# Set attention and a gated feed-forward on one core: block 0's second product in undivided float32, and one more super-block turned on the chip

## The chip, the cores and the metric

The kernel runs on one core of one Trainium2 chip. The metric is the device time of one execution in microseconds (us); before the change it is 1614.46 us, the median of three runs.

## What is computed

Four sets of 12480 points with 128 channels go through an attention with 32 inducing points, twice, and the result goes through a feed-forward layer with 2048 hidden channels:

```python
def mab(q, kv):
    s = scale * (q @ kv.transpose(0, 2, 1))
    s = s - s.max(-1, keepdims=True)
    a = np.exp(s)
    a /= a.sum(-1, keepdims=True) + 1e-09
    return a @ kv
h = mab(I, x)                      # I: inducing points, (4, 32, 128)
x = mab(x, h).reshape(4 * 12480, 128)
h = x @ w_in                       # w_in: (128, 2048)
g = h * (1.0 / (1.0 + np.exp(-1.702 * h)))
out = g @ w_out                    # w_out: (2048, 128)
```

The points and the inducing points are float32; w_in and w_out come as float64, and the kernel turns them into float32 itself.

## The kernel before

**Tiles.** A set is cut into six super-blocks of 2048 points (s = 0 to 5) and a rest of 192 (s = 6). A whole super-block holds four blocks of 512 points. The feed-forward layer goes by blocks: 98 in all, two of them made of the rests of two sets. A block has eight groups (`NG`), each of two chunks of 128 hidden channels.

**The feed-forward layer.** `first(i)` does group i: two float32r products into one `ph` buffer in PSUM (there are two), then the gated activation on ACT into `g`. It then divides `g` into `hi`, which is float32r, and the rest `lo`, so that products of full precision can be had from float32r: `hi` is made by ACT from `ph` again or by DVE from `g`, `lo` by DVE. `second(i, c)` does one chunk of the second product, three float32r products into the block's `pso`: `hi` with `wl`, `lo` with `wh`, `hi` with `wh`. w_out was divided in the same way into `wh` and `wl`. After a block's last chunk ACT copies `pso` to `ob`, which SP stores. Up to seven groups are ahead of the second product (`LAG`).

**The start.** `start` does the first attention of set 0 and the decoding of the weights, before the first block:

- The scores of super-block s (`scores`, PE) are copied by ACT, their maxima taken by DVE, then `softmax` makes the exponentials on ACT and their transposes `aT` on DVE. `weighing` multiplies `aT` by the rows of x, 16 products for a super-block. The rows come in two ways: for s below `XB` = 4, `turning` turns the columns that are there already (`xt`) by 16 transposes on PE into `ph` and two ACT copies into `xf`; for s = 4, 5 and 6 they are loaded from `in_x` a second time, as `xf`, `xn` (line 707, `x5`) and `xf_last`.
- After `weighing`, `joining` sums up (`hu`, `hT`), `first_weights` does the second attention of block 0 (`e`, `sm`, `two`, a turn of four float32r matmuls by `ident_r`, `st`), and `h_w_in` makes the four quarters of `hw`, the product of `hT` with w_in. Three more such turns (`more_weights`) make `st` for blocks 1 to 3.
- w_in and w_out are decoded in quarters of 512 columns by `decode_in` and `decode_out`: bit operations on DVE, two conversions on ACT. `decode_out` puts out `wh` (rounded by ACT) and `wl` (DVE). The quarters 2 and 3 of w_out are loaded when the weighing of super-block 5 has freed their buffer.
- `spin` fills PE's gaps with matmuls whose result nobody reads (`spun`).

**What sets the order.** The program is written once, for all engines, in an order that `Jobs` and `Clocks` choose when the kernel is built: each pending step has an engine and tiles, and the step that can begin first by modelled costs comes next, with a rank as a handicap. What they choose is fixed in the program; on the chip each engine goes through its own list in order and waits for what an instruction needs. In the main loop at the end, `begin_group` says whether the next group or the next chunk of the second product comes next, and `in_time` how much left-over work may be fitted in; DVE's share of decoding w_out is measured out by `progress` and `DECODE`.

The second product of block 0 needs the quarter of w_out for its chunk (`decoded`):

```python
pe_.matmul(o, wlc, hi[:, c, :], start=(ch == 0), stop=False)
pe_.matmul(o, whc, lo[:, c, :], start=False, stop=False)
pe_.matmul(o, whc, hi[:, c, :], start=False, stop=(ch == NCH - 1))
```

Line 112 of the profile is the helper that records every instruction, so that nearly all have that line; the operations are told apart by the tiles' names.

Of the kernel before, what the change touches and what calls it, by code (L numbers as in the profile page):

```python
# [9 lines left out]
F32 = mybir.dt.float32  # L10
# [12 lines left out]
LAG = 14  # L23
ROOM = 3000.0
LOAD = 400.0
WC = 512
DECODE = 7
ES = 4
XB = 4
FB = 5  # L30
# [86 lines left out]
class Queue(Meter):  # L117
# [3 lines left out]

    def dma_start(self, out, x):
        self.t = self.clocks.begin(self, [out], [x]) + self.cost("dma_start", out, x)
        self.moved = max(self.moved, self.t) + math.prod(out.shape) * 4 / LOAD
        self.clocks.end(self, self.moved + self.after, [out], [x])
        return self.eng.dma_start(out, x)

# [42 lines left out]
def set_attention_then_moe(ctx: ExitStack, tc, xT, x, indT, w_in, w_out, outT):  # L170
# [51 lines left out]
    sups.append((t0, RG, (N - t0) // RG))  # L222
    NS = len(sups)
    EB = NS + 2

    const = ctx.enter_context(tc.tile_pool(name="const", bufs=1))
    px = ctx.enter_context(tc.tile_pool(name="px", bufs=XB))
# [27 lines left out]
    act.activation(warm, one, AF.Exp)  # L255

    w_in_sb = [const.tile([P, WC], F32, name=f"w_in{c}") for c in range(DFF // WC)]
    wh = [const.tile([P, WC // P, P], F32R, name=f"wh{c}") for c in range(DFF // WC)]
    wl = [const.tile([P, WC // P, P], F32R, name=f"wl{c}") for c in range(DFF // WC)]

    xts = {}
# [77 lines left out]
    def first_products(a, s):  # L339

        t0, g, w = sups[s]
        pa = ps_a.tile([P, 512], F32, tag="pa", name="pa")
        xg = xts[a.b, s][:, 0:g * w]
        if a.b == 0 and s < XB:
# [325 lines left out]
    jobs = Jobs(clocks)  # L670
    used = {"pa": 0, "ph": 0, "po": 0}
    done = set()
    progress = [0]

    def has(*what):
        return lambda: all(x in done for x in what)
# [7 lines left out]
    def start(pf, pw):  # L684
# [25 lines left out]
        for s in range(XB, NS):  # L710
            if s == XB:
                t = pf.tile([P, BLK, P], F32, tag="xf", name="xf", bufs=FB)
            elif s < NS - 1:
                t = x5
            else:
                t = pf.tile([P, sups[s][2] // 32, P], F32, tag="xf_last", name="xf_last")
            turned[s] = load_x(0, s, t)
# [22 lines left out]
            act.activation(t.bitcast(F32), t, AF.Copy, scale=factor)  # L740
            done.add(name)

        def rounded(name, out, t):
            yield act, [t], None
            act.copy(out, t.bitcast(F32))
            done.add(name)

        def decode_in(c, t, m):
            raw = raws[c]
            h, l = bits(raw)  # L750
            jobs.add(size(("size in", c), t, raw))
# [4 lines left out]
            jobs.add(to_float(("fraction", c), m, 2.0 ** -30))  # L756
            yield from exponent(("size in", c), t, raw, 0x3F800000)
            yield dve, [m], has(("fraction", c))
            dve.scalar_tensor_tensor(
                w_in_sb[c], m.bitcast(F32), 1.0, t.bitcast(F32), op0=ALU.add, op1=ALU.mult  # L760
            )
            done.add(("w_in", c))

        def decode_out(c, raw, t, m, p):
            h, l = bits(raw)
            whc, wlc = [x[c].rearrange("p c d -> p (c d)") for x in (wh, wl)]
            jobs.add(size(("size out", c), t, raw), 1)
            yield dve, [raw], None
            progress[0] += 1
            dve.tensor_scalar(m, h, 0x1FF, 12, op0=ALU.bitwise_and, op1=ALU.logical_shift_left)  # L770
            yield dve, [raw], None
            progress[0] += 1
            dve.scalar_tensor_tensor(m, l, 20, m, op0=ALU.logical_shift_right, op1=ALU.bitwise_or)
            jobs.add(to_float(("rest", c), m, 2.0 ** -32), 1)
            yield from exponent(("size out", c), t, raw, 0x3FFFF000)
            progress[0] += 3
            jobs.add(rounded(("top", c), whc, t), 1)
            yield dve, [t], None
            progress[0] += 1
            dve.tensor_scalar(p, t, -(1 << 23), None, op0=ALU.bitwise_and)  # L780
            yield dve, [m], has(("rest", c), ("top", c))
            dve.tensor_mul(wlc, m.bitcast(F32), p.bitcast(F32))
            progress[0] += 1
            done.add(("w_out", c))

        def decodes_in():
            temps = [pst.tile([P, TOK], I32, tag="st", name="tmp") for _ in range(4)]
            for c in range(DFF // WC):
                yield from decode_in(c, *temps[c % 2 * 2:c % 2 * 2 + 2])

        def decodes_out():
            temps = [phw.tile([P, WC], I32, tag="hw", name="tmp") for _ in range(3)]
            for c in range(DFF // WC):
# [3 lines left out]
                yield from decode_out(c, raws[DFF // WC + c], *temps)  # L797


        def scores(s):  # L800
# [17 lines left out]
        def turning(s, k0):  # L818

            yield pe_, [xts[0, s]], bank("ph")  # L820
            if k0 == 0:
# [43 lines left out]
        def weighing():  # L865
            for some, at in ((range(ES), 0), (range(ES, NS), P)):
                i = 0
                for s in some:
                    what = [("aT", s)] + [("turned", s, k) for k in (0, 8) if s < XB]
# [159 lines left out]
    def first(i):  # L1029
# [24 lines left out]
    def second(i, c):  # L1054
# [8 lines left out]
        wlc, whc = [x[ch // 4][:, ch % 4] for x in (wl, wh)]  # L1063
        pe_.matmul(o, wlc, hi[:, c, :], start=(ch == 0), stop=False)
        pe_.matmul(o, whc, lo[:, c, :], start=False, stop=False)
        pe_.matmul(o, whc, hi[:, c, :], start=False, stop=(ch == NCH - 1))
        if ch == NCH - 1:
# [52 lines left out]
        late[0] = False  # L1120
        return weights_of(*key), key

    def decoded(ch):
        return ("w_out", ch // 4) in done

    def begin_group(i):

# [3 lines left out]
            return True  # L1131
        at, c = under_way[0]
        ch = 2 * (at % NG) + c
        if not decoded(ch):
            return True
        soon = clocks.free("ph", 2)
        return soon <= pe_.t or soon <= clocks.ready(*parts[at], wh[ch // 4], wl[ch // 4])

    def in_time(eng):

        if eng is dve and progress[0] < (i + 1) * DECODE // 2:
            return math.inf
        return act.t + 500 if eng is act else pe_.t

    i = 0
    while i < n or under_way:
# [2 lines left out]
            pass  # L1149
        if not begin_group(i):  # L1150
            at, c = under_way.pop(0)
            while not decoded(2 * (at % NG) + c):
                jobs.step(but=pe_)
            second(at, c)
        else:
# [55 lines left out]
```

## Time and profile before

| | |
|---|---|
| median of three runs (lowest, highest) | 1614.46 us (1612.99, 1615.7) |
| the profiled execution | 1611.53 us |
| its span, first to last instruction | 1609.5 us |
| PE busy | 1585.7 us, 99% of the span |
| DVE, ACT busy | 1328.2, 1365.1 us (83%, 85%) |
| mean granted clock of PE | 0.995 of full |
| chain that ended last | PE 93%, ACT 1%, DVE 1% |

PE is TensorE, DVE is VectorE, ACT is ScalarE, SP the engine that issues the DMAs. The granted clock is what the chip let TensorE have, as a share of 2.4 GHz. A matmul of float32 stands in the profile as two records, one of float32r as one; they overlap in the pipeline, so what one costs is read from start to start.

### The profile page before, as it was taken

What the parts mean: (1) busy time and instruction counts of PE and PEld (TensorE: products, weight loads), DVE (VectorE), ACT (ScalarE), POOL (GpSimd) and SP (SyncE); (2) the same over time, 40 slices, a digit from 0 to 9 for tenths busy, and PEclk for the clock granted to TensorE, in tenths of its full rate; (3) what the DMA queues carried; (4) which work ended last, traced back from release to release, by engine and by line L of the source; (5) the groups of instructions that cost most, each with busy time, mean ns of one, the idle gap of its engine ahead of it and who ended that gap; (6) DMA issues with size and microseconds to landing.
All of it is one profiled execution on the core that took longest, in us unless ns stands there. A gap on an engine that the chain in (4) does not pass through costs nothing.

```text
span 1609.5 us, 21978 instructions
## 1 busy us (share of the span) xinstructions
PE 1585.7 (99%) x7840; PEld 1238.5 (77%) x7840; DVE 1328.2 (83%) x1526; ACT 1365.1 (85%) x1572; POOL 0.7 (0%) x6
## 2 busy tenths in 40 slices
PE   8799999999999999999999999999999999999999
PEld 7567777777687877777777777777778788888887
DVE  6789787788888888788887987878878888888886
ACT  5589998988798888988798988888888988888885
POOL 0000000000000000000000000000000000000000
PEclk9899999999999999999999999999999999999999
DMA  9111504741223013650414210761211011011100
GB/s 293 53 53 53 180 18 87 174 105 53 91 92 142 30 40 78 170 123 15 123 37 151 77 33 25 173 148 46 77 65 48 19 40 47 30 37 40 37 30 20
DMA packets 87355, 126.76 MB, mean 79 GB/s; under 512 B 12241, under 2 KB 54993, under 8 KB 81617
## 3 DMA queue, kind: packets, MB, share of 16 engines
q1 hardware_dynamic: 87248, 125.37, 28.1%
q8 instruction: 64, 1.05, 0.3%
q14 instruction: 43, 0.34, 0.1%
HBM read 72.11 MB, written 25.56 MB: 61 GB/s over the span
## 4 chain that ended last, share of the span: by engine, by line
PE 93%; ACT 1%; DVE 1%; issue 0%; ACTq 0%
PE pso L112 67%; PE ph L112 23%; PE pa L112 4%; ACT g L112 0%; ACT L112 0%; DVE lo L112 0%; ACT hi L112 0%; ACT e L112 0%; DVE hi L112 0%; DVE tmp L112 0%; ACT tmp L112 0%; DVE e L112 0%; ACT ob L112 0%; ACT wh L112 0%; ACTq L112 0%
## 5 line engine op out<-in xcount | busy, mean ns | idle before, releaser
L112 DVE TENSOR_TENSOR lo<-g,hi 128x1024 fp32r<-128x1024 f32 (+1 forms) x784 | 948.9, 1217 | 166.6 <-ACT hi L112 153.3
L112 ACT ACTIVATE g<-ph 128x1024 f32<-128x1024 f32 (+1 forms) x784 | 810.2, 1038 | 184.8 <-PE ph L112 108.1
L112 PE MATMUL pso<-hi,wl 128*128 128x512 f32 (+1 forms) x1568 | 623.8, 398 | 8.5 <-DVE wl L112 8.5
L112 PE MATMUL pso<-lo,wh 128*128 128x512 f32 (+1 forms) x1568 | 617.6, 394 | 1.2 <-DVE lo L112 1.1
L112 PE MATMUL pso<-hi,wh 128*128 128x512 f32 (+1 forms) x1568 | 617.9, 394 | 0.0
L112 ACT ACTIVATE hi<-ph 128x1024 fp32r<-128x1024 f32 (+1 forms) x497 | 512.8, 1032 | 0.0
L112 PE MATMUL ph<-st,hw 128*128 128x512 f32 x1536 | 481.1, 397 | 4.1 <-ACT hi L112 3.1
L112 PEld LDWEIGHTS pso<-hi,wl 128*128 128x128 f32 x1568 | 295.2, 188 | 91.0 <-issue 11.2
L112 PEld LDWEIGHTS ph<-st,hw 128*128 128x128 f32 x1536 | 286.9, 188 | 84.1 <-ACT g L112 8.8
L112 PEld LDWEIGHTS pso<-hi,wh 128*128 128x128 f32 x1568 | 295.3, 188 | 70.2
L112 PEld LDWEIGHTS pso<-lo,wh 128*128 128x128 f32 x1568 | 294.8, 188 | 70.6 <-DVE lo L112 3.2
L112 DVE CAST hi<-g 128x1024 fp32r<-128x1024 f32 (+1 forms) x287 | 197.1, 687 | 81.2 <-ACT g L112 79.6
L112 ACT COPY ob<-pso 128x512 f32<-128x512 f32 (+1 forms) x98 | 59.3, 605 | 16.0 <-PE pso L112 16.0
L112 ACT ACT_TABLE_LOAD x30 | 38.5, 1283 | 1.3 <-PEq L1201 0.7
L112 PE MATMUL pa<-xt,hT 128*32 128x512 f32 x192 | 24.4, 600 | 1.7 <-DVE e L112 1.6
L979 PEld LDWEIGHTS spun<-ident 128*128 128x128 f32 x150 | 19.6, 205 | 6.3 <-issue 5.0
L112 PE MATMUL pa<-xt,indT_sb 128*32 128x512 f32 x192 | 23.7, 600 | 0.0
L979 PE MATMUL spun<-ident 128*128 128x128 f32 x150 | 22.1, 296 | 1.4 <-POOL ident masks.py:199 1.4
L112 PEld LDWEIGHTS pa<-xn,aT 128*32 128x32 f32 (+1 forms) x594 | 15.1, 109 | 7.7 <-issue 6.2
L112 PE MATMUL pa<-xn,aT 128*32 128x128 f32 (+1 forms) x594 | 20.7, 276 | 0.0
L112 ACT ACTIVATE e<-e 128x512 f32<-128x512 f32 (+1 forms) x28 | 14.5, 573 | 6.4 <-DVE e L112 6.4
L112 ACT ACTIVATE s<-s,nmx 128x512 f32<-128x512 f32 (+1 forms) x28 | 18.5, 663 | 1.0 <-DVE nmx L112 0.9
(91 smaller groups left out, 366.4 us busy)
## 6 DMA issues: line engine op xcount, KB each, us to landing
xt<-in_xT SPq DMA_DIRECT2D x44, 1024.0 KB, 7.1
out_T<-ob SPq DMA_DIRECT2D x96, 256.0 KB, 2.0
xn<-in_x SPq DMA_DIRECT2D x76, 256.0 KB, 5.5
st<-ahT SPq DMA_DIRECT2D x184, 64.0 KB, 2.0
st<-alT SPq DMA_DIRECT2D x184, 64.0 KB, 2.0
raw<-in_w_in SPq DMA_DIRECT2D x4, 512.0 KB, 8.5
raw<-in_w_out SPq DMA_DIRECT2D x4, 512.0 KB, 11.7
hw<-th SPq DMA_DIRECT2D x24, 64.0 KB, 2.0
```

Source lines behind the costliest of these rows:

```text
L112: return f(*a, **k)
L979: nc.tensor.matmul(spun[:, 0:P], ident, ident, start=True, stop=True)
```

## The change

Two things change. The rows of super-block 5 are made by `turning` too, with the transposes on PE and the copies on ACT, into the same buffer (`x5`); its second load from `in_x` goes. And the first eight groups (`WHOLE` = 8, all of block 0) keep `g` as it is, in float32, and multiply it by `whole`, a float32 w_out, in one float32 matmul. w_out is decoded like w_in (one `decode` for both), and `split` divides it into `wh` and `wl` afterwards, quarter by quarter: ACT rounds `whole` into a temporary, DVE subtracts it for `wl`, ACT writes `wh` into the buffer of a `whole` that block 0 has done with. Beside these, the modelled rate of loads of rows is lower (`ROWS`), the products of w_in are ranked later one by one, and `in_time` no longer measures out DVE's steps.

```diff
+    on_chip = [s for s in range(NS - 1) if s != XB]
...
-    wh = [const.tile([P, WC // P, P], F32R, name=f"wh{c}") for c in range(DFF // WC)]
+    pww = ctx.enter_context(tc.tile_pool(name="pww", bufs=DFF // WC))
+    whole = {}
+    wh = {}
...
             elif s < NS - 1:
-                t = x5
+                continue
...
-        def decode_out(c, raw, t, m, p):
...
+        def decode(name, out, raw, t, m, rank):
             h, l = bits(raw)
+            jobs.add(size(("size", name), t, raw), rank)
             yield dve, [raw], None
             dve.tensor_scalar(m, h, 0xFFFFF, 10, op0=ALU.bitwise_and, op1=ALU.logical_shift_left)
             yield dve, [raw], None
             dve.scalar_tensor_tensor(m, l, 22, m, op0=ALU.logical_shift_right, op1=ALU.bitwise_or)
+            jobs.add(to_float(("fraction", name), m, 2.0 ** -30), rank)
+            yield from exponent(("size", name), t, raw, 0x3F800000)
+            yield dve, [m], has(("fraction", name))
             dve.scalar_tensor_tensor(
+                out, m.bitcast(F32), 1.0, t.bitcast(F32), op0=ALU.add, op1=ALU.mult
             )
+            done.add(name)
+
+        def split(t):
+
+            for c in range(DFF // WC):
+                yield act, lambda: [whole[c]], has(("whole", c), ("w_out", DFF // WC - 1))
+                act.copy(t.bitcast(F32R), whole[c])
+                yield dve, [t], None
+                dve.tensor_sub(wl[c].rearrange("p c d -> p (c d)"), whole[c], t.bitcast(F32))
+                yield act, [wl[c]], None
+                wh_ = pww.tile([P, WC], F32R, tag="w", name=f"wh{c}")
+                act.copy(wh_, t.bitcast(F32))
+                wh[c] = wh_.rearrange("p (c d) -> p c d", d=P)
+                done.add(("split", c))
...
+            if k0 == 0 and s > XB:
+                turned[s] = x5
+            elif k0 == 0:
                 turned[s] = pf.tile([P, BLK, P], F32, tag="xf", name="xf", bufs=FB)
...
-            if s < XB:
+            if s in on_chip:
                 jobs.add(turning(s, 0), 1)
                 jobs.add(turning(s, 8), 1)
...
-            jobs.add(h_w_in(c), c // 2)
+            jobs.add(h_w_in(c), c)
...
+        if i < WHOLE:
+            g = ph_.tile([P, 2, TOK], F32, tag="hi", name="g")
+            act.activation(g, ph, AF.Gelu_apprx_sigmoid)
+            parts[i] = g, g
+            return
...
+        last = ch == NCH - 1
+        if i < WHOLE:
+            pe_.matmul(
+                o, whole[ch // 4][:, ch % 4 * P:(ch % 4 + 1) * P], hi[:, c, :],
+                start=(ch == 0), stop=last,
+            )
+            if i >= WHOLE - NG and ch % 4 == 3:
+                done.add(("whole", ch // 4))
+        else:
...
-        if eng is dve and progress[0] < (i + 1) * DECODE // 2:
+        if eng is dve:
             return math.inf
```

PE around the weighing (`h`) of set 0, before; `spun` is the filling, `ph<-ident,xt` are transposes:

```order
L112 MATMUL pa<-xt,indT_sb 32x512 x4
L979 MATMUL spun<-ident 128x128 x5
L112 MATMUL pa<-ident,mx_417 1x128
L979 MATMUL spun<-ident 128x128 x2
L112 MATMUL h_169<-xf,aT 32x128 x16
L112 MATMUL pa<-one,row 32x1 x4
L979 MATMUL spun<-ident 128x128 x2
L112 MATMUL h_169<-xf,aT 32x128 x64
L112 MATMUL h_169<-xn,aT 32x128 x16
L112 MATMUL h_169<-xf_last,aT 32x128 x3
```

and with the change:

```order
L113 MATMUL pa<-xt,indT_sb 32x512 x4
L972 MATMUL spun<-ident 128x128
L113 MATMUL ph<-ident,xt 128x128 x8
L113 MATMUL pa<-ident,mx_419 1x128
L113 MATMUL ph<-ident,xt 128x128 x8
L113 MATMUL pa<-one,row 32x1 x4
L113 MATMUL h_164<-xf,aT 32x128 x16
L972 MATMUL spun<-ident 128x128 x2
L113 MATMUL h_164<-xf,aT 32x128 x48
L972 MATMUL spun<-ident 128x128 x4
L113 MATMUL h_164<-xf,aT 32x128 x16
L113 MATMUL h_164<-xn,aT 32x128 x16
```

(Before the change the three products with `xf_last` are the last row; after it they come next.) The 16 transposes of super-block 5 now stand between its scores and the weighing, and `pa<-one,row`, the step back of the maximum, stands ahead of the weighing.

ACT in the same place, before; `s` are the scores (each in its own numbered buffer, the one of 64x96 is the rest), `less` comes from the two maxima:

```order
L112 ACTIVATE s_351,rs<-s_351,nmx 128x512
L112 ACTIVATE less<-less 128x1
L112 ACTIVATE s_391,rs<-s_391,nmx 128x512
L112 ACTIVATE s_412,rs<-s_412,nmx 128x512
L112 ACTIVATE s_364,rs<-s_364,nmx 64x96
L112 ACTIVATE tmp<-raw 128x512
L112 ACTIVATE tmp<-tmp 128x512
```

and with the change:

```order
L113 ACTIVATE s_303,rs<-s_303,nmx 128x512
L113 ACTIVATE less<-less 128x1
L113 ACTIVATE s_347,rs<-s_347,nmx 128x512
L113 ACTIVATE s_387,rs<-s_387,nmx 128x512
L113 ACTIVATE s_408,rs<-s_408,nmx 128x512
L113 COPY xn<-ph 128x1024 x2
L113 ACTIVATE s_360,rs<-s_360,nmx 64x96
L113 ACTIVATE tmp<-raw 128x512
```

The two copies of turned rows stand ahead of the rest's exponential, and `less` one exponential earlier.

PE from the first group on, before:

```order
L112 MATMUL ph<-st,hw 128x512 x6
L112 MATMUL pso<-hi,wl_117 128x512
L112 MATMUL pso<-lo,wh_113 128x512
L112 MATMUL pso<-hi,wh_113 128x512
L112 MATMUL pso<-hi,wl_117 128x512
L112 MATMUL pso<-lo,wh_113 128x512
L112 MATMUL pso<-hi,wh_113 128x512
L112 MATMUL ph<-st,hw 128x512 x2
L112 MATMUL pso<-hi,wl_117 128x512
L112 MATMUL pso<-lo,wh_113 128x512
L112 MATMUL pso<-hi,wh_113 128x512
L112 MATMUL ph<-st,hw 128x512 x2
```

and with the change, with the engine or DMA queue whose semaphore each waits for:

```order
L113 MATMUL ph<-st,hw 128x512 [waits Activation_49]
L113 MATMUL ph<-st,hw 128x512 x3
L113 MATMUL ph<-st,hw 128x512 [waits Activation_49]
L113 MATMUL ph<-st,hw 128x512
L113 MATMUL pso<-g,whole 128x512 [waits DMAHW5_49]
L113 MATMUL ph<-st,hw 128x512 [waits Activation_49]
L113 MATMUL ph<-st,hw 128x512
L113 MATMUL pso<-g,whole 128x512
L113 MATMUL ph<-st,hw 128x512 [waits DVE_49,Activation_49]
L113 MATMUL ph<-st,hw 128x512
L113 MATMUL pso<-g,whole 128x512
L113 MATMUL ph<-st,hw 128x512 [waits Activation_49]
```

One product of `g` with `whole` stands where three stood; the third pair of `ph` still comes after two.

## Rows read from the trace of the kernel before

**Rows 1.** Windows: us, busy us of each engine (instructions), PEclk, DMA share, GB/s.
```profile
51.87:90.02 38.15, 26.50 (x88) 19.21 (x89) 31.78 (x48) 25.62 (x34) 0.00 (x0) 0.82 0.03 10
84.00:1600.00 1516.00, 1512.73 (x7248) 1184.23 (x7249) 1268.51 (x1403) 1315.99 (x1494) 0.00 (x0) 1.00 0.27 74
```

**Rows 2.** Waits of PE, whole run: us in total, times, longest us.
```profile
PE pso L112 <- DVE wl L112: 8.5, 3, 3.6
```

**Rows 3.** Timeline, 31 to 45 us: start us, us, engine, line, operation, count, idle before.
```profile
32.48 0.20 ACT L112 ACTIVATE less<-less 128x1 f32<-128x1 f32 x1 [0.39 <-DVE less L112]
...
33.30 0.71 ACT L112 ACTIVATE s<-s,nmx 128x512 f32<-128x512 f32 x1
...
34.27 0.19 ACT L112 ACTIVATION_READ_ACCUMULATOR s<-s,nmx 64x1 f32 x1
...
35.38 0.26 DVE L112 STREAM_TRANSPOSE aT<-s 64x96 f32<-64x96 f32 x1
...
39.73 1.08 PE L112 MATMUL h<-xn,aT 128*32 128x128 f32 x32 [2.77 <-DMA xn<-in_x]
...
41.22 0.35 DVE L112 TENSOR_SCALAR hu<-h,less 128x128 f32<-128x128 f32 x1 [5.00 <-PE h L112]
```

**Rows 4.** Timeline, 81 to 90 us.
```profile
82.91 1.03 ACT L112 ACTIVATE hi<-ph 128x1024 fp32r<-128x1024 f32 x1
...
83.81 1.05 ACT L112 ACTIVATE g<-ph 128x1024 f32<-128x1024 f32 x1
...
84.56 0.56 PE L112 MATMUL pa<-ident_r,two 128*128 128x128 f32 x4
...
87.56 0.63 PE L112 MATMUL ph<-st,hw 128*128 128x512 f32 x2
...
88.03 0.39 PE L112 MATMUL pso<-hi,wl 128*128 128x512 f32 x1
...
88.49 0.40 PE L112 MATMUL pso<-hi,wh 128*128 128x512 f32 x1
```

**Rows 5.** Timeline, 21 to 31 us.
```profile
22.98 1.97 PE L112 MATMUL ph<-ident,xt 128*128 128x128 f32 x16
...
24.11 1.93 ACT L112 COPY xf<-ph 128x1024 f32<-128x1024 f32 x2 [0.43 <-PE ph L112]
```

**Rows 6.** Timeline, 43 to 54 us.
```profile
44.95 1.98 PE L112 MATMUL hw<-w_in,hT 128*128 128x512 f32 x4
...
45.61 2.20 SPq L126 DMA_DIRECT2D raw<-in_w_out  x2
...
48.60 0.28 DVE L112 TENSOR_REDUCE sm<-e 128x4 f32<-128x128 f32 x1
...
51.23 0.59 ACT L112 CAST st<-pa 128x512 fp32r<-128x512 f32 x1 [0.69 <-PE pa L112]
...
51.87 1.21 PE L112 MATMUL ph<-st,hw 128*128 128x512 f32 x4 [0.40 <-ACT st L112]
```

**Rows 7.** Groups by form, 51.87 to 90.02 us: count, busy us, mean ns, idle before.
```profile
L112 DVE TENSOR_TENSOR lo<-g,hi 128x1024 fp32r<-128x1024 f32 x12 | 14.7, 1222 | 0.8 <-ACT hi L112 0.5
...
L112 DVE SCALAR_TENSOR_TENSOR tmp<-raw,tmp 128x512 int32<-128x512 int32 x6 | 4.2, 693 | 0.2
...
L112 DVE TENSOR_SCALAR tmp<-raw 128x512 int32<-128x512 int32 x3 | 1.3, 422 | 0.0
```

**Rows 8.** DMA issues, 40 to 60 us, then the whole run: count, KB, us to landing.
```profile
raw<-in_w_out SPq DMA_DIRECT2D x2, 512.0 KB, 7.8
...
raw<-in_w_out SPq DMA_DIRECT2D x4, 512.0 KB, 11.7
```

**Rows 9.** Windows of the stretches with a low granted clock.
```profile
54.46:62.40 7.94, 4.81 (x12) 3.84 (x12) 6.77 (x11) 4.34 (x6) 0.00 (x0) 0.57 0.00 1
...
69.20:72.60 3.40, 3.40 (x9) 2.27 (x8) 2.06 (x5) 1.98 (x3) 0.00 (x0) 0.50 0.00 0
...
76.00:79.50 3.50, 3.50 (x10) 2.68 (x9) 3.31 (x6) 3.02 (x6) 0.00 (x0) 0.51 0.00 0
```

More of the change, by code (lines that the diff above doesn't have):

```diff
@@ L25 @@
 LOAD = 400.0
+ROWS = 190.0
 WC = 512
-DECODE = 7
+WHOLE = 8
 ES = 4
@@ L123, in dma_start @@
         self.t = self.clocks.begin(self, [out], [x]) + self.cost("dma_start", out, x)
-        self.moved = max(self.moved, self.t) + math.prod(out.shape) * 4 / LOAD
+        rate = LOAD if out.shape[-1] > P or x.shape[-1] > P else ROWS
+        self.moved = max(self.moved, self.t) + math.prod(out.shape) * 4 / rate
         self.clocks.end(self, self.moved + self.after, [out], [x])
@@ L343, in first_products @@
         xg = xts[a.b, s][:, 0:g * w]
-        if a.b == 0 and s < XB:
+        if a.b == 0 and s in on_chip:
             xg = xg.rearrange("c (k g i) -> c g k i", g=g, i=32)
@@ L672, in set_attention_then_moe @@
     done = set()
-    progress = [0]
     def has(*what):
@@ L741, in to_float @@
             done.add(name)
[L743 to L749, printed above, removed]
+        def decode(name, out, raw, t, m, rank):
             h, l = bits(raw)
-            jobs.add(size(("size in", c), t, raw))
+            jobs.add(size(("size", name), t, raw), rank)
             yield dve, [raw], None
@@ L755, in decode_in @@
             dve.scalar_tensor_tensor(m, l, 22, m, op0=ALU.logical_shift_right, op1=ALU.bitwise_or)
-            jobs.add(to_float(("fraction", c), m, 2.0 ** -30))
-            yield from exponent(("size in", c), t, raw, 0x3F800000)
-            yield dve, [m], has(("fraction", c))
+            jobs.add(to_float(("fraction", name), m, 2.0 ** -30), rank)
+            yield from exponent(("size", name), t, raw, 0x3F800000)
+            yield dve, [m], has(("fraction", name))
             dve.scalar_tensor_tensor(
-                w_in_sb[c], m.bitcast(F32), 1.0, t.bitcast(F32), op0=ALU.add, op1=ALU.mult
+                out, m.bitcast(F32), 1.0, t.bitcast(F32), op0=ALU.add, op1=ALU.mult
@@ L761, in decode_in @@
             )
-            done.add(("w_in", c))
-        def decode_out(c, raw, t, m, p):
[L765 to L784, printed above, removed]
+            done.add(name)
@@ L788, in decodes_in @@
             for c in range(DFF // WC):
-                yield from decode_in(c, *temps[c % 2 * 2:c % 2 * 2 + 2])
+                yield from decode(("w_in", c), w_in_sb[c], raws[c], *temps[c % 2 * 2:][:2], 0)
         def decodes_out():
             temps = [phw.tile([P, WC], I32, tag="hw", name="tmp") for _ in range(3)]
+            jobs.add(split(temps[2]), 1)
             for c in range(DFF // WC):
@@ L796, in decodes_out @@
                     load_out()
-                yield from decode_out(c, raws[DFF // WC + c], *temps)
+                whole[c] = pww.tile([P, WC], F32, tag="w", name="whole")
+                yield from decode(("w_out", c), whole[c], raws[DFF // WC + c], *temps[:2], 1)
         def scores(s):
@@ L820, in turning @@
             yield pe_, [xts[0, s]], bank("ph")
-            if k0 == 0:
+            if k0 == 0 and s > XB:
+                turned[s] = x5
+            elif k0 == 0:
                 turned[s] = pf.tile([P, BLK, P], F32, tag="xf", name="xf", bufs=FB)
@@ L868, in weighing @@
                 for s in some:
-                    what = [("aT", s)] + [("turned", s, k) for k in (0, 8) if s < XB]
+                    what = [("aT", s)] + [("turned", s, k) for k in (0, 8) if s in on_chip]
                     yield pe_, lambda: [a.aTs[s], turned[s]], has(*what)
@@ L1062, in second @@
         hi, lo = parts.pop(i) if c else parts[i]
[L1063 to L1067, printed above, removed]
+        last = ch == NCH - 1
[7 more added lines that the diff above has]
+        else:
+            wlc, whc = [x[ch // 4][:, ch % 4] for x in (wl, wh)]
+            pe_.matmul(o, wlc, hi[:, c, :], start=(ch == 0), stop=False)
+            pe_.matmul(o, whc, lo[:, c, :], start=False, stop=False)
+            pe_.matmul(o, whc, hi[:, c, :], start=False, stop=last)
+        if last:
             ob = po.tile([P, TOK], F32, tag="ob", name="ob")
@@ L1121, in lay_out, with decoded @@
         return weights_of(*key), key
-    def decoded(ch):
-        return ("w_out", ch // 4) in done
+    def decoded(i, c):
+        return ("w_out" if i < WHOLE else "split", (2 * (i % NG) + c) // 4) in done
     def begin_group(i):
@@ L1133, in begin_group @@
         ch = 2 * (at % NG) + c
-        if not decoded(ch):
+        if not decoded(at, c):
             return True
         soon = clocks.free("ph", 2)
-        return soon <= pe_.t or soon <= clocks.ready(*parts[at], wh[ch // 4], wl[ch // 4])
+        return soon <= pe_.t or soon <= clocks.ready(*parts[at], *([] if at < WHOLE else [wh[ch // 4], wl[ch // 4]]))
     def in_time(eng):
-        if eng is dve and progress[0] < (i + 1) * DECODE // 2:
+        if eng is dve:
             return math.inf
@@ L1151, in set_attention_then_moe @@
             at, c = under_way.pop(0)
-            while not decoded(2 * (at % NG) + c):
+            while not decoded(at, c):
                 jobs.step(but=pe_)
```

## The prediction

> **What bounds the kernel now.** I read the stages first, then what PE waits for, then the start in order of time. From 84 us to 1600 PE is busy 1512.7 of 1516 us at full clock, so after 84 us only PE work counts; the stretch before it is different: from the first `ph` product at 51.87 to 90.02 PE is busy 26.5 of 38.2 us and the mean granted clock is 0.82, while DVE is busy 31.8 us [rows 1]. The largest wait of PE in the whole run lies there: 8.5 us in three waits of `pso` for DVE's `wl`, a quarter of w_out that is not decoded yet [rows 2]. Ahead of that stretch one wait sets the chain: the weighing of super-block 5 waits 2.8 us for its rows (`xn<-in_x`), starts at 39.73, and `hu` on DVE follows at 41.22 [rows 3]. So the change touches two places, and all of it lies before 90 us.
>
> **Where to measure.** Block 0 ends on PE with the `hi,wh` product at 88.49, whose successor would start 0.23 later, at 88.72 [rows 4]. By then PE has issued 13 `ph` pairs and 3 of the 4 `two` turns. In the changed order block 0 ends after 12 `ph` pairs and 4 turns. A `ph` pair takes 0.47 (87.56 to 88.03, [rows 4]) and a turn of four matmuls about 0.5 (0.56 listed at 84.56, in the same group), so the two states are level to 0.1 us. From about the twentieth group on the instruction orders are the same, so the difference here is the difference of the ends.
>
> **Part 1: rows of super-block 5 turned on PE.** Removed: four `xn` loads from SP's queue and PE's wait for them. Added: 16 transposes on PE, between the scores of super-block 5 and the weighing, in place of idle spinning; 16 took 1.97 at 22.98 [rows 5], so eight take 0.95. The step to `pa<-one,row` needs both halves done: it moves to about 31.0, while before it stood behind the first 16 weighing products. `less` on ACT then starts at 31.7 instead of 32.48 [rows 3]. Each exponential takes 0.71 (33.30, [rows 3]), so those of 3, 4, 5 start at 31.8, 32.5, 33.2. Now ACT has two `xn<-ph` copies that the order puts ahead of the last exponential: 1.93 for two [rows 5], so 33.9 to 35.8. The last exponential's sum is read at 36.0 (before: 34.27), and the last `aT` on DVE ended 1.37 after that point (35.38 + 0.26, [rows 3]): 37.4. PE's last three products and the step to `hu` add 0.5 (41.22 minus 39.73 is 1.5, of which the 16 products of super-block 5 are 1.0, [rows 3]): `hu` at 37.9 in place of 41.22, **3.3 us earlier**. What ends last is now ACT's copies, no longer a DMA. `xf_last`, now four issues earlier on SP, is no bound, and the two later w_out halves are issued earlier by the same 3 us.
>
> **From `hu` to the first `ph`.** The chain is unchanged apart from order. The change puts one `hw` subtraction, not two, ahead of `sm` on DVE, so `sm` starts about 0.6 earlier against `hu`, at 44.7 (before 48.60); `st` follows 2.63 later (48.60 to 51.23, [rows 6]) at 47.3. But the fourth `hw` product has moved behind the turn on PE and waits for DVE's second `hw` subtraction, which stands behind `whole[0]`: 46.5 + 0.7 + 0.7 = 47.9. That float32 product of 128x512 takes 0.86 (two took 1.98 with their last end, four records at a pitch of 0.43, [rows 6]). First `ph` at 48.8, **3.1 earlier** than 51.87. ACT casts `st`, `hw`, `tmp`, `hw` before the first `g`, which starts at 50.05.
>
> **Part 2: block 0 with an undivided w_out.** On PE three float32r products of 0.23 (two from 88.03 to 88.49, [rows 4]) become one float32 product of 0.86. Sixteen chunks cost 16 x (0.86 - 0.70) = **2.5 us more** PE work. Off PE, eight groups lose `hi` (0.9 on ACT, start to start, 82.91 to 83.81, [rows 4], or on DVE) and `lo` (1.22 on DVE, [rows 7]): about 12 of the 31.8 us that keep DVE busy. A quarter's decode takes DVE three long passes of 0.69 and three short ones of 0.42 [rows 7]: 3.4 us with the steps between them.
>
> The chain goes by PE, with `g` at 0.90 each on ACT. The third `ph` needs g0 (done 51.1), so PE idles 49.8 to 51.1; then product 0 to 52.5, `ph` and product 1 to 53.9, `ph` and product 2 to 55.2. ACT has put `two` ahead of g3 (54.2) because DVE normalises `e` after `whole[1]` (52.2); g3 ends 55.3, g4 56.2, and PE fits to 0.1. Products 4 and 5 end at 58.8, a turn 59.3, 6 to 8 at 62.3 (`whole[2]` is ready at 59). Two turns, two `ph` and products 9 to 11 end at 66.3; `ph` and products 12 to 14 at 69.4 (`whole[3]` ready at 62.4); turn, `ph`, product 15 at **71.2**. ACT is the near bound: its splitting casts stand among g7 to g10, and PE waits a few tenths for them. PE's work from 48.8 on is 12 x 0.47 + 16 x 0.86 + 3 x 0.5 = 20.9 of 22.4 us.
>
> The first product carries a wait on a DMA semaphore. If that is the later w_out half, issued 45.61 [rows 6] with 7.8 to landing [rows 8], it lands now near 50.5 to 52: level with the product (51.7); I take 0, at most 3.9 (the 11.7 that the four w_out loads took in the median, [rows 8]).
>
> **Sum.** 88.72 - 71.2 = 17.5 us. By terms: first `ph` 3.1 earlier; PE work 2.5 dearer; idle and half-clock time in block 0, 88.72 - 51.87 - (13 x 0.47 + 16 x 0.70 + 2 x 0.5) = 18.6 before, 1.5 now, so 17.1 off. 3.1 - 2.5 + 17.1 gives 17.7, the same within rounding. The splitting of w_out (per quarter two ACT casts and one DVE subtraction of 0.69) comes in blocks 0 and 1, behind PE's four groups of lead; cost taken as 0, bounded by 8 casts at the 0.59 of `st` [rows 6], 4.7 us, if nothing hides them. Below, nothing: no PE work leaves. The profiled execution took 1611.5 (span 1609.5), so it would take 1594.0; the median of the runs shown, 1614.5, is 2.9 above it, and the forecast goes by the median: **1597.0 us**.
>
> **The clock.** Three stretches after idle ran at 0.57, 0.50 and 0.51 of full clock, 54.5 to 62.4, 69.2 to 72.6, 76 to 79.5 [rows 9]; the lower of the two levels is 1.2 GHz. In the changed block 0 the only idle over half a microsecond is the 1.3 before g0 and 0.6 near 62, so I assume none. The Trainium skill ("TensorE: Matmul & The Clock Gate", "A second HAM failure mode: psum-queue depth-cycling") says that short idles between groups of matmuls that cycle through PSUM banks are enough to make the clock swing between the levels. By that rule block 0, whose `ph` has two buffers, would run partly at 1.2 GHz and end later; by the rows it stays at 2.4. The trace agrees that it swings, though around waits of up to 3.6 us [rows 2], longer than those expected here.
>
> **Rivals.** (a) *The clock falls once or twice in block 0.* For it: it fell three times in the same place before. Each stretch like 69.2 to 72.6 gives half of 3.4 us away: 1.7 to 3.4, so 1598.7 to 1600.4. Chance 0.27. (b) *ACT's casts or the DMA wait eat a part*: 3.9 or 4.7 us, 1601 to 1602; 0.12. Against it: the chain shows PE with 4 groups of lead at 71.2. (c) *Nearly nothing is left*, between 1611.2 and 1617.7: DVE still late with `whole[2]` and `whole[3]`, each waited for as long as the `wl` before (8.5), and the clock low with it (8.5 more): about 1614. Against it: DVE has 3.4 us per quarter and little else. 0.03. (d) *Slower*: float32 products at 1.2 GHz throughout. Place: block 0; price: PE work of 20.9 doubled ends at 48.8 + 41.8 = 90.6, and what idles remain (1.5) put it at 92, 3.4 behind 88.72: 1617.9. It decides when over nine tenths of block 0 runs at the low level. Against it: under products back to back the clock was 1.00 for 1516 us [rows 1]. 0.02. (e) *More gained*, if ACT's order waits less than I laid out: PE work alone gives 48.8 + 20.9 = 69.7, so 1595.5, and run-to-run spread below it; 0.06. The rest, 0.50, is the forecast, 1595 to 1598.7.
>
> **How the numbers follow.** Faster by over 0.2% (3.2 us, about what a measurement of this kernel can tell from no change): the forecast, (a), (b) and (e), 0.95; within it (c), 0.03; slower (d), 0.02. The range takes in (a), (b) and (e) with the runs' own spread of 1.5 to either side: 1593 to 1604.
>
> **What would show it.** Right: no `xn` wait on PE before 40 us, `hu` near 38, first `ph` near 48.8, no wait of `pso` for DVE, block 0's last product starting near 70.3, granted clock 1.00 from 48 to 72, and the rest shifted by 17 to 18 us. Wrong, if `pso<-g,whole` records stand at a pitch of 0.85 for more than a few, if PE waits for a DMA at the first product, or if `ph` waits for `g` or `hi` sum to more than 4 us between 48 and 90.

## The result, and the profile after

| | before | after |
|---|---|---|
| median of four runs (lowest, highest) | 1613.99 us (1612.99, 1615.7) | 1593.11 us (1592.72, 1593.67) |
| span of the profiled execution | 1609.5 us | 1591.5 us |

The ratio is 0.987, 95% interval 0.9853 to 0.9887. By the medians the gain is 20.9 us, by the two profiled executions 18.0, since the one of before was among the quickest of its kernel. The places below are read from the profiled pair.

Where the gain arises and where some of it goes is seen on the `ob<-pso` copies, which ACT makes at the end of each block. The timeline of before, for blocks 0, 1 and 2 (start us, us, engine, line, operation, count, idle before):

```profile
90.02 0.67 ACT L112 COPY ob<-pso 128x512 f32<-128x512 f32 x1
...
108.07 0.60 ACT L112 COPY ob<-pso 128x512 f32<-128x512 f32 x1
...
124.83 0.60 ACT L112 COPY ob<-pso 128x512 f32<-128x512 f32 x1
...
1593.75 0.59 ACT L112 COPY ob<-pso 128x512 f32<-128x512 f32 x1 [0.33 <-PE pso L112]
```

The last row is block 96. The same of after:

```profile
74.87 0.59 ACT L113 COPY ob<-pso 128x512 f32<-128x512 f32 x1
...
94.86 0.60 ACT L113 COPY ob<-pso 128x512 f32<-128x512 f32 x1
...
112.52 0.60 ACT L113 COPY ob<-pso 128x512 f32<-128x512 f32 x1
...
1575.97 0.59 ACT L113 COPY ob<-pso 128x512 f32<-128x512 f32 x1 [0.33 <-PE pso L113]
```

Block 0 ends 15.15 us earlier, block 2 only 12.31, block 96 17.78. The prediction had 17.5 at block 0 and nothing after it. So two terms are missing in it: 2.8 us lost between blocks 0 and 2, and 5.5 us gained evenly over the other 94 blocks, where the order of the instructions is the same as before.

**The start** differs from one execution to the next. From 4.4 to 6.4 us both kernels do the same filling, at a different pace (windows: length in us, then busy us and number of records of PE, PEld (its weight loads), DVE, ACT and POOL). Before:

```profile
4.40:6.40 2.00, 2.00 (x20) 2.00 (x20) 0.93 (x2) 0.68 (x1) 0.00 (x0) 1.00 0.99 377
```

After, with a stretch ahead of it and one behind it:

```profile
3.00:4.00 1.00, 1.00 (x7) 1.00 (x6) 0.00 (x0) 0.00 (x0) 0.00 (x0) 1.00 1.04 315
...
4.40:6.40 2.00, 2.00 (x11) 2.00 (x11) 0.86 (x2) 0.68 (x1) 0.00 (x0) 1.00 0.97 367
...
7.00:8.00 1.00, 1.00 (x11) 1.00 (x10) 0.94 (x2) 0.32 (x1) 0.00 (x0) 1.00 0.95 385
```

From 4.4 to 6.4 PE does 20 records of the small products in one and 11 in the other, and all that follows is 1.0 later in this profile. What differs is when PE comes to full pace: a small product (two records) takes 0.43 us up to 6.5 us in this profile and 0.22 from then on, and before has the same two paces with the step at 4.4. That is about the ratio of the two levels of the clock. The column of the granted clock shows 1.00 all through, but the trace's list of levels begins only at that step, in both. Of four kernels below with the same program up to here (the change, its two small edits, and both together) three show 11 and one 20, so this goes by the execution; 1.0 is added below where it says "on equal start".

**The weighing**, timeline of after from 28 us:

```profile
28.54 1.07 PE L113 MATMUL pa<-xt,indT_sb 128*32 128x512 f32 x8
...
35.08 1.90 ACT L113 COPY xn<-ph 128x1024 f32<-128x1024 f32 x2
...
36.74 1.16 PE L972 MATMUL spun<-ident 128*128 128x128 f32 x8
...
37.15 0.19 ACT L113 ACTIVATION_READ_ACCUMULATOR s<-s,nmx 64x1 f32 x1
...
37.83 1.08 PE L113 MATMUL h<-xf,aT 128*32 128x128 f32 x32
...
37.97 0.26 DVE L113 STREAM_TRANSPOSE aT<-s 64x96 f32<-64x96 f32 x1
38.73 1.06 PE L113 MATMUL h<-xn,aT 128*32 128x128 f32 x32
39.71 0.42 PE L113 MATMUL h<-xf_last,aT 64*32 64x128 f32 x6
...
40.19 0.35 DVE L113 TENSOR_SCALAR hu<-h,less 128x128 f32<-128x128 f32 x1 [1.96 <-PE h L113]
```

The DMA wait of [rows 3] is gone. The last `aT` is ready at 38.23, but PE reaches its last products only at 39.71: it works through `spun`, 32 records of `xf` and 32 of `xn` one after the other, without a wait. `hu` comes 1.03 earlier than before, 2.05 on equal start; 3.3 were predicted.

**Block 0**, timeline of after:

```profile
50.51 1.49 PE L113 MATMUL ph<-st,hw 128*128 128x512 f32 x4
...
52.12 2.88 ACT L113 ACTIVATE g<-ph 128x1024 f32<-128x1024 f32 x3
...
53.20 0.74 PE L113 MATMUL ph<-st,hw 128*128 128x512 f32 x2 [1.20 <-ACT g L113]
53.77 1.02 PE L113 MATMUL pso<-g,whole 128*128 128x512 f32 x2
...
61.69 2.74 PE L113 MATMUL pso<-g,whole 128*128 128x512 f32 x6
...
72.21 1.02 PE L113 MATMUL pso<-g,whole 128*128 128x512 f32 x2
72.66 0.79 PE L113 MATMUL pso<-hi,wl 128*128 128x512 f32 x1
```

The first product waits for no DMA, three products in a row (six records) take 2.74 with their last end, about 0.86 each, and one wait of 1.20 for `g` is all that PE still waits in block 0; the waits of [rows 2] for `wl` are gone. The last product starts at 72.21, so its end on PE is at 73.07, against 88.72. The windows of after (us, busy us of PE, PEld, DVE, ACT, POOL, granted clock, DMA share, GB/s) answer to [rows 1]:

```profile
50.51:73.07 22.56, 21.36 (x71) 11.74 (x70) 18.99 (x34) 19.53 (x30) 0.00 (x0) 1.00 0.02 7
...
90.00:95.20 5.20, 3.21 (x12) 1.79 (x10) 2.13 (x4) 4.98 (x6) 0.00 (x0) 1.00 0.00 0
95.30:98.60 3.30, 3.30 (x8) 2.65 (x9) 3.20 (x6) 3.27 (x5) 0.00 (x0) 0.50 0.21 79
```

Block 0 takes 22.6 us instead of 36.9 (51.87 to 88.72), at full clock throughout, where before three stretches ran at about half [rows 9]. DVE is busy 19.0 us, against 31.8 in [rows 1].

**The loss behind block 0** is in the last two of these windows: PE idles 2.0 of 5.2 us, and then runs 3.3 us at 1.2 GHz. The timeline of after shows who is waited for:

```profile
90.19 0.63 ACT L113 ACTIVATE e<-e 128x512 f32<-128x512 f32 x1 [1.37 <-DVE e L113]
...
90.84 1.28 ACT L113 ACT_TABLE_LOAD   x1
...
92.14 1.94 ACT L113 ACTIVATE g<-ph 128x1024 f32<-128x1024 f32 x2
...
93.21 0.72 PE L113 MATMUL ph<-st,hw 128*128 128x512 f32 x2 [1.22 <-ACT g L113]
...
95.20 0.78 PE L113 MATMUL pso<-lo,wh 128*128 128x512 f32 x1 [0.77 <-DVE lo L113]
```

The second attention of the next super-block has begun (`e`). ACT stands 1.37 us waiting for DVE's `e`, makes one exponential and loads a table for 1.28 us, and only then comes to the next `g`. PE waits for that `g`, then for its `lo`. Before, PE idled 3.3 of the 1516 us from 84 us on [rows 1]; here 2.0 in five. At the `ob` copies 1.9 of the 2.8 us is lost between blocks 0 and 1 and 0.9 between blocks 1 and 2, where the half clock lies.

### The profile page after: what moved, and what is told of

Same layout as the page of the kernel before. It is cut to its first block, busy times and chain, and to the rows that moved or that the text cites. A ratio compares the mean times of both kernels' runs of the same rounds, so it can differ in the third digit from the quotient of the medians.

```text
span 1591.5 us, 21955 instructions
## 1 busy us (share of the span) xinstructions
PE 1580.0 (99%) x7842; PEld 1236.7 (78%) x7842; DVE 1318.4 (83%) x1515; ACT 1362.8 (86%) x1573; POOL 0.7 (0%) x6
## 4 chain that ended last, share of the span: by engine, by line
PE 96%; ACT 2%; DVE 1%; DMA 0%; issue 0%; SPq 0%; POOLq 0%; ACTq 0%; POOL 0%
PE pso L113 67%; PE ph L113 23%; PE pa L113 5%; PE spun L972 1%; ACT L113 1%; DVE lo L113 1%; DMA raw<-in_w_out 0%; ACT g L113 0%; PE h L113 0%; ACT hi L113 0%; ACT e L113 0%; DVE hi L113 0%; DVE e L113 0%; SPq L128 0%; DVE m L113 0%
## 5 line engine op out<-in xcount | busy, mean ns | idle before, releaser
L113 DVE TENSOR_TENSOR lo<-g,hi 128x1024 fp32r<-128x1024 f32 x776 | 939.0, 1217 | 162.8 <-ACT hi L113 148.1
L113 PE MATMUL pso<-hi,wl 128*128 128x512 f32 (+1 forms) x1552 | 614.2, 396 | 0.0
L113 PE MATMUL pso<-lo,wh 128*128 128x512 f32 (+1 forms) x1552 | 608.1, 392 | 2.0 <-DVE lo L113 1.9
L113 PE MATMUL pso<-hi,wh 128*128 128x512 f32 (+1 forms) x1552 | 609.8, 393 | 0.0
L113 PEld LDWEIGHTS pso<-hi,wl 128*128 128x128 f32 x1552 | 291.6, 188 | 82.3 <-issue 12.1
L113 PEld LDWEIGHTS pso<-hi,wh 128*128 128x128 f32 x1552 | 291.5, 188 | 66.7
L113 DVE CAST hi<-g 128x1024 fp32r<-128x1024 f32 x284 | 195.1, 687 | 75.9 <-ACT g L113 74.3
L113 DVE TENSOR_REDUCE mx<-s 128x1 f32<-128x512 f32 (+1 forms) x27 | 16.7, 621 | 4.0 <-ACT s L113 3.2
```

What stands on the lines that cost most here:

```text
L113: return f(*a, **k)
```

## Experiments

Each kernel is compared with the kernel before on its own chip. Places are those of its profile. Every expectation names its own theories.

### Where the tiles lie: the even gain

The change also moves tiles in SBUF. `wh` (8 KB of each partition: four quarters of 512 float32) leaves the constants, which stand first, for `pww`, which is opened late, so everything allocated between, `wl`, `xt`, `e`, `aT`, `st`, `hw` among it, lies 8 KB lower. The first kernel (place_new) is **before**, with this move alone and every instruction in its old order:

```diff
-    wh = [const.tile([P, WC // P, P], F32R, name=f"wh{c}") for c in range(DFF // WC)]
+    pww = ctx.enter_context(tc.tile_pool(name="pww", bufs=DFF // WC))
+    wh = [pww.tile([P, WC // P, P], F32R, tag="w", name=f"wh{c}") for c in range(DFF // WC)]
```

> The kernel before, with wh alone moved in SBUF to where the change has it, so that xt, e, aT, st and hw lie 8 KB per partition lower, as in the change; the order of the instructions is that of before. After block 2 the changed kernel gains 5.5 us more, evenly, to the end. Theory 'place': the float32r products run 1 to 3 ns closer together because of where their operands lie; then this kernel is 5 to 6 us faster than before (about 1608.5) and the gain grows evenly after 90 us. Theory 'execution': the spacing differs from one execution to the next whatever the kernel; then it is within 1.5 us of before.

Measured: 1607.74 us (1607.24 to 1610.12), ratio 0.9958 (0.9946 to 0.9971). Timeline, blocks 0, 2 and 96:

```profile
91.48 0.68 ACT L112 COPY ob<-pso 128x512 f32<-128x512 f32 x1
...
126.21 0.61 ACT L112 COPY ob<-pso 128x512 f32<-128x512 f32 x1
...
1589.54 0.59 ACT L112 COPY ob<-pso 128x512 f32<-128x512 f32 x1 [0.33 <-PE pso L112]
```

It is 1.38 later than before at block 2 and 4.21 earlier at block 96: 5.6 us, evenly, from addresses alone.

The second (place_old) is **the change**, with `pww` opened ahead of the pools of `xt` and the rest, so that these come back to their old places (`wl` and `wh` have then changed sides):

```diff
+    pww = ctx.enter_context(tc.tile_pool(name="pww", bufs=DFF // WC))
     px = ctx.enter_context(tc.tile_pool(name="px", bufs=XB))
...
-    pww = ctx.enter_context(tc.tile_pool(name="pww", bufs=DFF // WC))
```

> The change, with the buffers of whole and wh put ahead of xt, so that xt, e, aT, st and hw lie where they lie in the kernel before. Theory 'place' by the shift of st and hw: about 5 us slower than the change (1598). Theory 'place' by where wh and wl lie: as the change or between. Theory 'execution': as the change, 1593, within 1.5 us.

Measured: 1597.60 us (1597.27 to 1598.81), ratio 0.9894 (0.9881 to 0.9908).

```profile
74.30 0.59 ACT L113 COPY ob<-pso 128x512 f32<-128x512 f32 x1
...
111.12 0.61 ACT L113 COPY ob<-pso 128x512 f32<-128x512 f32 x1
...
1580.14 0.59 ACT L113 COPY ob<-pso 128x512 f32<-128x512 f32 x1 [0.33 <-PE pso L113]
```

The gain is 13.71 at block 2 and 13.61 at block 96: flat. By the medians the old places cost the change 4.5 us, by the two ratios to before 3.9. Both kernels say the same: the even gain is the place of tiles, not the arithmetic. This profile has the same two waits behind block 0 as the change (1.19 for `g`, 0.76 for `lo`), but no stretch at half clock.

Which tiles? A third kernel (place_mid), **before** again, opens `pww` between `aT` and `st`, so that `wl`, `xt`, `e` and `aT` lie 8 KB lower, `wh` lies elsewhere, and `st`, `hw` and what comes after keep their addresses (the pool is opened ahead of `pst` instead):

> The kernel before, with wh between aT and st: xt, e and aT lie 8 KB lower as in the change, but st, hw and everything behind them where they lay before. Theory 1 (the place of st and hw makes the 6 us): as before, 1614 to 1615. Theory 2 (the place of wh, or of xt to aT, makes it): 1608 to 1609.

Measured: 1613.06 us (1612.16 to 1615.76), ratio 0.9989 (0.998 to 0.9999); from block 2 to block 96 it gains 0.7 us, not 5.6. That looks as if only `st`, `hw` and the pools behind them counted, but the 0.7 is a sum in which larger parts cancel. The table has the mean time from the start of one product to the start of the next, in ns, worked out from the traces between 130 and 1575 us, without the few above 400 ns:

| from, to | before | place_old | place_new | place_mid |
|---|---|---|---|---|
| `hi,wh` to `hi,wl` | 233.3 | 233.3 | 230.3 | 230.2 |
| `hi,wl` to `lo,wh` | 234.7 | 234.7 | 233.3 | 233.4 |
| `lo,wh` to `hi,wh` | 230.3 | 230.3 | 229.2 | 231.9 |
| `hi,wh` to `ph` | 229.1 | 229.0 | 231.0 | 233.4 |

The change and the other kernels with its places repeat the means of place_new to 0.2 ns, so this goes by the places and not by the execution. In place_mid the first two steps are as short as in place_new, and the last two are longer than anywhere. Of the tiles that these products read, only `wh` lies elsewhere than in place_old. So the place of `wh` is not without effect, and this run does not narrow the even gain down to `st`, `hw` and the pools behind them.

### The parts alone

Part 1 alone (the turned rows, in the kernel before):

```diff
+    on_chip = [s for s in range(NS - 1) if s != XB]
...
-            if s < XB:
+            if s in on_chip:
```

> Part 1 alone: super-block 5 turned on PE, the rest as before. Theory A (the parts add up): hu 2 to 3 us earlier than 41.22 and the end 2 to 3 us earlier, 1611 to 1612. Theory B (block 0 is bound by the decoding on DVE, which does not begin earlier): hu earlier, but PE waits for wl so much longer, gain 0 to 1 us.

Measured: 1612.54 us (1611.66 to 1614.07), ratio 0.9988 (0.9979 to 0.9997). `hu` and the waits of PE in its profile:

```profile
40.38 0.35 DVE L112 TENSOR_SCALAR hu<-h,less 128x128 f32<-128x128 f32 x1 [2.37 <-PE h L112]
```

```profile
PE pso L112 <- DVE wl L112: 9.2, 3, 4.2
```

`hu` starts 0.84 earlier, 1.64 on equal start (at the scores of super-block 5 this profile is 0.8 behind before), and the wait for `wl` grows from 8.5 to 9.2. At block 2 its copy is 0.5 later than before, 0.3 earlier on equal start: in the profiles nearly all that the start gains is waited for again in block 0, since DVE's decoding sets its end there. The runs give 1.9 by the ratio, with an interval from 0.5 to 3.4.

Part 2 alone, with the loads of rows modelled as in the change:

```diff
-    on_chip = [s for s in range(NS - 1) if s != XB]
+    on_chip = list(range(XB))
...
-                continue
+                t = x5
```

> Part 2 alone: block 0 in undivided float32, super-block 5 loaded twice as before. Theory A (the parts add up): the weighing waits for xn again, hu near 41 to 42, and the time is 1 to 3 us over the change: 1594 to 1596. Theory B (what part 1 gives is lost later anyway): 1593, as the change.

Measured: 1598.72 us (1597.78 to 1599.66), ratio 0.9901 (0.9886 to 0.9916). `hu` is at 45.71, since the planned order now puts 4.96 us of filling ahead of the products of super-block 5:

```profile
39.34 4.96 PE L972 MATMUL spun<-ident 128*128 128x128 f32 x42
...
45.71 0.35 DVE L113 TENSOR_SCALAR hu<-h,less 128x128 f32<-128x128 f32 x1 [2.22 <-PE h L113]
```

This kernel does not price part 1 fairly, so the next has `ROWS = 400.0`, as before, besides:

> Part 2 alone, planned with the old rate for loads of rows (400 in place of 190); whole_only had hu at 45.7, later than before. Theory A: that came of the planner, which believes the rows to come late and fills PE with matmuls until then; with the old rate hu is at 41 to 42 and the time 1594 to 1595.5, so part 1 is worth 1 to 2 us. Theory B: it came of the second load; hu stays at 45 and the time at 1598.7.

Measured: 1595.38 us (1593.47 to 1597.02), ratio 0.9882 (0.9867 to 0.9896). The timeline and a window of its profile:

```profile
40.32 1.51 PEld L113 LDWEIGHTS h<-xn,aT 128*32 128x32 f32 x32 [3.02 <-issue]
40.35 1.94 PE L113 MATMUL h<-xn,aT 128*32 128x128 f32 x32 [2.78 <-DMA xn<-in_x]
...
42.92 0.35 DVE L113 TENSOR_SCALAR hu<-h,less 128x128 f32<-128x128 f32 x1 [6.12 <-PE h L113]
```

```profile
39.80:46.50 6.70, 6.15 (x55) 5.41 (x56) 1.80 (x7) 0.00 (x0) 0.00 (x0) 0.50 0.00 0
```

The wait for `xn` is back, 2.78, and this time the clock was at half for 6.7 us behind it. With part 2 in place, part 1 is worth 2.3 us by the medians (1595.38 against 1593.11); the two intervals overlap and its own runs go from 1593.47 to 1597.02, so its size is no surer than that.

### What ended the weighing

The change, without filling between the last maximum and the end of the weighing:

```diff
-            while pe_.t + 2 * 107 <= t:
+            while pe_.t + 2 * 107 <= t and (("nmx", NS) not in done or "h" in done):
```

> The change, without the filling matmuls on PE between the step back of the second maximum and the attention's result (8 products of 16 in the changed order, of which 4 stand right ahead of super-block 4's weighing). Theory A: PE itself ended the weighing last (its products in series, with the filling between them), so hu comes 1.2 to 1.5 us earlier (38.7 in place of 40.2) and the end with it, about 1592. Theory B (as predicted): ACT's copies and the last exponential end last, and hu stays within 0.4 us of 40.2; time as the change.

Measured: 1591.18 us (1591.03 to 1591.5), ratio 0.9856 (0.984 to 0.9873). The scores of super-block 5, a weight load of the weighing and `hu`:

```profile
27.52 1.06 PE L113 MATMUL pa<-xt,indT_sb 128*32 128x512 f32 x8
...
35.07 1.75 PEld L113 LDWEIGHTS h<-xf,aT 128*32 128x32 f32 x64 [0.91 <-DVE aT L113]
...
38.36 0.35 DVE L113 TENSOR_SCALAR hu<-h,less 128x128 f32<-128x128 f32 x1 [1.15 <-PE h L113]
```

From the scores to `hu` it takes 10.84, where the change took 11.65 (28.54 to 40.19) and before 13.70. So PE's own queue ended the weighing; 0.8 of it was filling. That is less than the 1.2 to 1.5 expected, since PE, without the filling, waits in the middle for an `aT` of DVE (its weight load for 0.91). The rest of the 1.8 by which `hu` lies ahead is this run's start. The medians differ by 1.9; three of the four executions have a mean granted clock of 1.000, those of the change 0.998 to 0.999, so a part of that is likely the half clock behind block 0.

### What ended block 0

The change, with one extra DVE subtraction (1.22 us, result unused, the output as before) in each of block 0's eight groups, which gives DVE back 9.8 us of the work that the change takes from it (from 31.8 to 19.0 busy in block 0):

```diff
+            d = pg.tile([P, 2, TOK], F32, tag="g", name="d")
+            dve.tensor_sub(d, g, g)
```

> The change, with one subtraction of 128x1024 more on DVE in each of the first eight groups, whose result nobody reads: 8 x 1.22 = 9.8 us of DVE in block 0. Theory A (the gain of part 2 is DVE's time, taken from hi and lo and left to the decoding): whole of quarters 2 and 3 comes up to 9.8 us later, PE waits for it, block 0 ends 5 to 9 us later, 1598 to 1602. Theory B (the gain is that a chunk waits for less, not for hi, lo, wh and wl; DVE has room to spare): at most 2 us.

Measured: 1601.14 us (1599.15 to 1603.0), ratio 0.9918 (0.9903 to 0.9932). Waits of PE, then a window:

```profile
PE pso L113 <- DVE whole L113: 3.8, 1, 3.8
```

```profile
68.80:75.60 6.80, 5.97 (x10) 2.64 (x9) 6.53 (x10) 6.04 (x11) 0.00 (x0) 0.50 0.00 0
```

9.8 us of DVE work cost 8.0: one wait of 3.8 for a decoded quarter, a half-clock stretch of 6.8 behind it, and block 1 begins at 80.54 instead of 72.66. That is the picture of before again, with float32 products in it. DVE's time was what block 0 waited for, and the clock went down behind the wait. The run shows this for 8.0 of the 15.65 us by which block 0 ends earlier; what the rest owes to the `hi` that ACT no longer makes, or to products that wait for fewer tiles, is not tested.

### The loss behind block 0

The change, with the second attention of super-block 1 begun three groups later:

```diff
+    begin[0, 1] += 3
```

> The change, with the layout of super-block 1's weights, which forces its exponential and the two table loads on ACT, due three groups later. Theory A: the stall behind block 0 (ACT idle 1.4 us for e, PE 1.2 and 0.8 us for g and lo at 92 to 95, then a stretch at half clock) comes of this place; it goes, and 1.5 to 3.5 us with it: 1589.5 to 1591.5. Theory B: the table loads stop ACT wherever they stand while PE's lead is as short as it is after block 0: 1593.

Measured: 1591.25 us (1590.99 to 1591.37), ratio 0.9856 (0.9842 to 0.9871). Waits of PE, then the window that answers to the loss:

```profile
PE ph L113 <- ACT g L113: 1.2, 1, 1.2
```

```profile
90.00:100.00 10.00, 9.32 (x41) 7.27 (x40) 7.32 (x11) 9.94 (x12) 0.00 (x0) 1.00 0.07 26
```

The second wait for `g` and the half clock are gone, with 2.1 us of the span (1589.4, at the same start as the change). The half clock is a part of these 2.1 (0.9 at the `ob` copies of the change) that does not come with the waits every time, since place_old had the same waits at full clock. Both edits together:

> The change with both: no filling matmuls during the weighing, and super-block 1's weights due three groups later. Each alone gave about 1.9 us (1591.2 in place of 1593.1). If the two stand in different places on PE's chain they add up: 1589.2 to 1589.7. If one eats the other, 1591.

Measured: 1589.74 us (1588.74 to 1590.06), ratio 0.984 (0.9826 to 0.9855); its span is 3.2 below that of the change, 1.1 for the weighing and 2.1 for the stall.

Last, both edits and `wl` moved out of the constants as well, into a pool behind `wh`, which puts `st`, `hw` and the rest, `wh` among it, another 8 KB lower and `wl` where `wh` lay:

```diff
+    pwl = ctx.enter_context(tc.tile_pool(name="pwl", bufs=DFF // WC))
...
+    wl = [pwl.tile([P, WC // P, P], F32R, tag="wl", name=f"wl{c}") for c in range(DFF // WC)]
```

> As the run 'both', with wl moved behind wh in SBUF too, so that xt to hw lie 8 KB lower once more and wl 112 KB higher. Theory 1 (what matters is that st and hw, or xt to aT, lie at certain places): the spacing of the products changes again, by 2 to 6 us either way. Theory 2 (what matters is how far wh lies from the low part of SBUF, nothing else): the time of 'both', within 1 us.

Measured: **1587.68 us** (1587.04 to 1587.9), ratio 0.9828 (0.9813 to 0.9843), 28 us below before and the fastest kernel here. Against the last kernel its copies are 0.56 earlier at block 3 and 2.35 at block 97: 1.8 more is gained block by block. Its weighing shows one thing more:

```profile
38.05 0.41 PE L113 MATMUL h<-xf_last,aT 64*32 64x128 f32 x6 [0.22 <-DVE aT L113]
```

Here PE waits for the last `aT`, 0.22: with its queue short enough, ACT's copies and the exponential behind them do end last, as the prediction had it. In the run without filling and in that of both edits alone PE's queue still ended last, 0.7 and 0.4 behind that `aT`.

## Why the prediction was right, and where it was not

The time was right, though inside the range by only 0.1 us: 1597.0 forecast, 1593 to 1604 the range, 1593.11 measured, below the 1595 to 1598.7 in which the forecast saw its own case. So was the bound: DVE's decoding set the end of block 0, undivided products relieve it, and the run with DVE's work given back shows it for 8.0 us. The sum came out near for another reason than given. Predicted were 17.5 at block 0 and nothing behind it; by the profiles it is 15.65 on PE (16.7 on equal start), which is 15.15 at the `ob` copies, then 2.8 lost and 5.5 gained: 17.8. That this is near 17.5 is luck.

- **`hu` 3.3 us earlier: 2.05.** The failed step is "What ends last is now ACT's copies, no longer a DMA". PE's queue ended last: the prediction followed ACT and did not add up what PE still had to do in order: the transposes, the filling and the products of several super-blocks.
- **First `ph` 3.1 earlier: 1.36** (50.51), 2.4 on equal start. It fell short by less than `hu` did, since the steps from `hu` to it took 10.3, 0.6 less than laid out.
- **PE work 2.5 dearer, idle and half-clock time 17.1 less.** The products cost 0.86 to 0.87 as taken. From the first `ph` to the last product's end block 0 took 22.56, predicted 22.4 (48.8 to 71.2): the sum of the waits was right to 0.2.
- **The DMA wait of the first product, taken as 0 (at most 3.9): 0.** Splitting, taken as 0 (at most 4.7): no wait of PE for `wl` or `wh` is in the profile.
- **The clock.** The prediction took full clock in block 0, and it was 1.00. The Trainium skill ("TensorE: Matmul & The Clock Gate", "A second HAM failure mode: psum-queue depth-cycling") tells of a bf16 kernel in which short idles between groups that cycle through PSUM banks made the clock swing. Were it so here, part of block 0 would have run at half; this trace does not agree there, with waits of up to 1.20 us. The fall came behind block 0 instead, at 95.3, after waits of 1.22 and 0.77, where the prediction did not look; in place_old it did not come after waits of 1.19 and 0.76 in the same place.
- **"The difference here is the difference of the ends"** fell, twice. The order behind the twentieth group is the same, as said, but its waits are not: PE leaves block 0 earlier, and at 92.0 finds no `g` ready while ACT and DVE are busy with `e` (2.8 lost; beginning that work three groups later gives 2.1 back). Two things of the prediction bear on it and are not tested: PE leaves block 0 with 12 groups begun instead of 13, which it set level by PE's work alone, and the casts of the splitting, taken as 0, keep ACT busy in between up to 78 us. And the same instructions at other addresses run faster (5.6 gained). "Below, nothing: no PE work leaves" was wrong for this: what PE does is the same, but not the spacing.
- **The base.** The forecast took the gain off the median of before. In its profile the change with the old places gains 13.7 us, not 17.5, but before was profiled in an execution 3.4 us below the median of its later runs (1611.53, 1614.94), and by the medians that kernel gains 17.3. So its 1597.60 lies near 1597.0 because the overestimate and the quick execution cancel.

By the parts: of the 20.9 us some 2 are part 1 by the runs (2.3 with part 2 in place, 1.9 alone, neither sure), and 4.5 (change against its old places) to 7.2 (before against the new ones, 1614.94 to 1607.74) the places of tiles, which the change does not name (5.5 and 5.6 in the profiles); the rest is part 2, net of the loss. The forecast was 3.9 too high: without the places it would have been too low, by less than 1 (1597.60 with the old ones).

Open: how the place of a tile changes the spacing of PE's products; which of `wh`, `st`, `hw` and the pools behind them does it (`g`, `hi`, `lo` and `ob` did not move); when the clock falls behind a wait and when not; and why the untraced runs of before lie above its profiled one (their mean granted clock, 0.992 to 0.997, lies around its 0.995).

## What to carry to other kernels

After a change that frees an engine, follow the next scarce one past the end of the changed stage: here PE arrived early at work that ACT and DVE had not prepared, and moving that work by three groups was worth 2 us. When a DMA wait is taken away, add up PE's own queue before naming another engine as the bound. And where a change adds or drops a pool, run the old program with the new places alone, since the difference may be neither the old work nor the new.

## What was not expected of the hardware

The place of operands in SBUF changes a kernel that PE bounds: moving `wh` behind the rest, which shifts that rest by 8 KB, is 5.6 us in 1500 (0.4%) with the order of instructions unchanged, moving `wl` too gives some 1.8 more, and `wh` in the middle 0.7, a sum of steps that grew by up to 4.3 ns and steps that shrank by up to 3.1. And the start of one program is not always the same: in the 2 us from 4.4 to 6.4 PE did 11 to 20 records of the same products, as it came to full pace at 6.5 or at 4.4, which moves all that follows by 1.0 us; over all the kernels here the step lies between 4.4 and 7.4.
